# Sweeps over pairs of tiles: 512-column matmuls in place of 256-column ones, with partial sums in joint buffers

## The chip, the cores and the metric

The kernel runs on one core of a Trainium2 chip. A core has five engines with a queue of instructions each: TensorE (PE in the profile, its weight loads PEld), VectorE (DVE), ScalarE (ACT), GpSimd (POOL) and SyncE (SP), which here only issues DMA transfers. TensorE reads SBUF and writes PSUM, whose banks hold 512 float32 columns of 128 partitions. The metric is the device time of one execution in microseconds (us), and the median of several runs is compared.

## What is computed

A chunked linear attention feeds a feed-forward layer. There are 4 batches, 8 heads, 768 positions, a head size of 32 and a state of 16, so 3072 tokens of 256 features reach the second part, which has 2048 hidden features.

```python
for c in range(nc):                       # attention, chunk by chunk
    L = np.exp(cum[:, :, :, None] - cum[:, :, None, :]) * causal
    M = np.einsum('bhin,bhjn->bhij', Cc, Bc) * L
    y[:, :, sl] = M @ xc + np.einsum('bhin,bhnd->bhid', Cc, state) * decay_to_i
    state = decay_full * state + sum_j(Bc[j] * xc[j] * decay_from_j)
x = y.transpose(0, 2, 1, 3).reshape(3072, 256)
h = x @ w_in                              # 256 -> 2048
g = h - np.tanh(h)
out = g @ w_out                           # 2048 -> 256
```

All inputs are float32, except that the two weight matrices come as float64.

## The kernel before

Tokens are columns. The feed-forward part takes them in eight tiles (`WIDTH`, line 31): tiles 0 to 3 have 256 columns, tiles 4 to 7 have 512. The hidden features are 16 blocks f of 128, two to a weight pair u = f // 2.

**A step** (t, f) works on one bank of hidden values. `mm1` (735) computes ph, `act` (773) makes g = ph - tanh(ph) with ScalarE (785) and VectorE (789), and splits g into a rounded part gh (ScalarE, 793) and a rest gl (VectorE, 799). `mm2` (809) multiplies these by the second weights and adds to the output bank or banks `po`. A product of rounded operands is three matmuls, (wh, gh), (wl, gh) and (wh, gl), and in the same way for x in mm1 (755, 831). `blocks(t)` (732) says how many blocks f fit in a bank: for a tile of 256 columns two, so that a step holds 12 matmuls of 256 columns in mm1 and 12 in mm2; for a tile of 512 columns one, and 6 of 512 columns in each. A narrow tile has both output halves e = 0, 1 in the one bank po0; a wide one has them in po0 and po1 (`banks`, 813). Each of the two has one buffer; ph has two (`NPH`).

**Sweeps.** The weights arrive one pair after another and are converted from float64 bits on the way (`conv`). So that work can start early, the narrow tiles are gone through four times (`SWEEPS`, line 53): in the first sweep each takes f = 0 to 3, then each takes 4 to 7, and so on (1075). Partial outputs are put by: after the first sweep `keep` (850) copies the bank into a buffer `pt`, one for each tile; after each later one `add` (863) copies it into a buffer `ob` (two in turn) and an accumulating DMA issued by GpSimd adds that to `pt`. After the last, `store` (875) sends `pt` out in two halves. Tiles 4 to 7 then run all 16 blocks in one go, evicted by ScalarE (e = 0) and VectorE (e = 1). In the first sweep some work runs on unsplit float32 operands (`plain`, `native`: 749, 825).

**Attention.** 28 chunks of up to 112 columns deliver x. Early ones (below `JOINT` = 10) have a bank po1 or po0 for their y (617); later ones come in pairs and take a ph bank (683). Where a chunk is planned is set by `at_` (1093 to 1104). The columns of x lie in a ring: those of tile 5 overwrite those of tiles 0 and 1, so the chunks concerned (12 and 13 first) wait until the last mm1 on the old columns (`over`, 415).

**Order.** Nothing runs as it is written. Each piece of work is recorded with an engine, an estimated cost and its dependencies (`Order`, 59), slots of buffers in the order in which they are asked for. `search` (194 to 207) simulates the whole list 16 times with priorities from the longest remaining path plus a random jitter of fixed seed, and the best order is issued. Mm2 is recorded two steps behind mm1 (`LAG`).

Of the kernel before, what the change touches and what calls it, by code (L numbers as in the profile page):

```python
# [10 lines left out]
F32 = mybir.dt.float32  # L11
# [5 lines left out]
ALU = mybir.AluOpType  # L17
# [3 lines left out]
P = 128  # L21
# [4 lines left out]
NF = FF // P  # L26
# [3 lines left out]
NCK = NB * CPB  # L30
WIDTH = 256, 256, 256, 256, 512, 512, 512, 512
NSW = 4
NT = len(WIDTH)
START = [sum(WIDTH[:t]) for t in range(NT + 1)]
BANK = 512
QLEN = [QL if k >= NCK - NB else Q for k in range(NCK)]
OFF = [sum(QLEN[:k]) for k in range(NCK + 1)]
RING = START[NSW] + WIDTH[NSW]
COL = [START[t] if t <= NSW else START[t] - START[NSW + 1] for t in range(NT)]
CPG = 2  # L40
NG = NCK // CPG
NCONV = NF // 2
# [10 lines left out]
SWEEPS = 0, 2, 4, 6, 8  # L53
# [5 lines left out]
class Order:  # L59
# [1 line left out]


    DMA_LATENCY, SEM, SEM_PE, RATE, FLIGHT = 0.8, 0.15, 0.28, 0.32e6, 8
    ROUNDS, JITTER, SEED, EARLY, LOOK = 16, 0.3, 143, 8.0, 0.5

    def __init__(self):
        self.ops, self.urge = [], []
# [4 lines left out]
    def slot(self, tag, bufs):  # L72
        k = self.count[tag] = self.count.get(tag, -1) + 1
        self.fresh[f"{tag}#{k}"] = tag, f"{tag}#{k - bufs}"
        return f"{tag}#{k}"
# [142 lines left out]
def tile_ssm_moe(ctx: ExitStack, tc: tile.TileContext, a, x, bn, bc, wts, out):  # L218
# [22 lines left out]
    chunks = {t: [k for k in range(NCK) if (START[t] <= OFF[k] or t == 0) and OFF[k] < START[t + 1]] for t in range(NT)}  # L241
    wv, wm, pts, n_pt = {}, {}, {}, {}
    mm1s = {t: [] for t in range(NT)}
    KB = P * 1024

    JOINT = chunks[NSW][0] // CPG * CPG
# [164 lines left out]
    def over(ts, col, w):  # L411

        old = {o for o in range(max(ts)) if max(ts) > NSW and o not in ts and COL[o] < col + w and col < COL[o] + WIDTH[o]}
        assert all(len(mm1s[o]) == NF // blocks(o) for o in old)
        return [i for o in old for i in mm1s[o]]

    def group(G):
# [309 lines left out]


    def rate(w):
        return w * (0.2352 / 512 if 2 * w > BANK else 0.1178 / 256) / 2  # L730

    def blocks(t):
        return BANK // WIDTH[t]

    def mm1(t, f):
        w = WIDTH[t]
        ts = slice(COL[t], COL[t] + w)
        n = [f"x{e}{k}@{t}" for k in range(NCK) if OFF[k] < START[t] + w and OFF[k + 1] > START[t] for e in "hl"]
        n_h, n_g = slot("ph", NPH), slot("g", 3)
        gs[t, f, 0] = [n_h, n_g]  # L740

        def fn():
            ph = ps_h.tile([P, BANK], F32, tag="ph", name=f"ph{t}_{f}")
            gs[t, f] = [ph]
            for i in range(blocks(t)):
                u, j = divmod(f + i, 2)
                if plain(t, f):
                    for k in range(2):
                        nc.tensor.matmul(out=ph[:, i * w : i * w + w], lhsT=part(slice(0, 1), wv[u]).rearrange(  # L749
                                             "p i (k c) -> p (i k) c", k=2)[:, k, j * P : (j + 1) * P],  # L750
                                         rhs=xf[:, k, START[t] : START[t] + w], start=k == 0, stop=k == 1, skip_group_check=True)
                    continue
                for p in range(2):
                    for k in range(2):
                        for w_ in (wh, wl)[: 2 - p]:
                            nc.tensor.matmul(out=ph[:, i * w : i * w + w], lhsT=w_[:, u, 0, k, j * P : (j + 1) * P],  # L756
                                             rhs=(xh, xl)[p][:, k, ts], start=p == 0 and k == 0 and w_ is wh,
                                             stop=p == 1 and k == 1, skip_group_check=True)

        mm1s[t].append(len(op.ops))  # L760
        if plain(t, f):
            n = sorted({"xf" + k[2:] for k in n})
            op("PE", 14.6 * rate(w) * blocks(t), fn, r=[*n, convs[f // 2]], w=[n_h])
            return
        op("PE", 12 * rate(w) * blocks(t), fn, r=[*n, f"wh{f // 2}.0", f"wl{f // 2}.0"], w=[n_h])

# [5 lines left out]

    def act(t, f):
        n_h, n_g = gs[t, f, 0]
        used = WIDTH[t] * blocks(t)
        if native(t, f):
            gs[t, f, 0] += [n_g]
        else:
            n_gh, n_gl = slot("gh", 3), slot("gl", 3)
            gs[t, f, 0] += [n_gh, n_gl]  # L780

        def fn_t():
            g = p3.tile([P, BANK], F32, tag="g", name=f"g{t}_{f}")
            gs[t, f].append(g)
            nc.scalar.activation(g[:, 0:used], gs[t, f][0][:, 0:used], AF.Tanh)  # L785

        def fn_s():
            ph, g = (v[:, 0:used] for v in gs[t, f])
            nc.vector.tensor_tensor(out=g, in0=ph, in1=g, op=ALU.subtract)  # L789

        def fn_h():
            gh = pg.tile([P, BANK], F32R, tag="gh", name=f"gh{t}_{f}")
            nc.scalar.copy(gh[:, 0:used], gs[t, f][1][:, 0:used])  # L793
            gs[t, f].append(gh)

        def fn_l():
            _, g, gh = gs[t, f]
            gl = pg.tile([P, BANK], F32R, tag="gl", name=f"gl{t}_{f}")
            nc.vector.tensor_tensor(out=gl[:, 0:used], in0=g[:, 0:used], in1=gh[:, 0:used].bitcast(F32), op=ALU.subtract)  # L799
            gs[t, f].append(gl)  # L800

        op("ACT", 0.6, fn_t, r=[n_h], w=[n_g])
        op("DVE", 0.69, fn_s, r=[n_h], w=[n_g])
        if native(t, f):
            return
        op("ACT", 0.62, fn_h, r=[n_g], w=[n_gh])
        op("DVE", 0.71, fn_l, r=[n_g, n_gh], w=[n_gl])

    def mm2(t, f, seg):

        w, last = WIDTH[t], f + blocks(t) == seg[1]
        _, _, *n_in = gs[t, f, 0]
        banks = 1 if 2 * w <= BANK else 2
        if f == seg[0]:
# [23 lines left out]
                                             stop=last and k == 2 and i == blocks(t) - 1, skip_group_check=True)  # L838

        if native(t, f):  # L840
            op("PE", 14.5 * rate(w) * blocks(t), fn, r=[*n_in, f"wf{f // 2}"], w=n_po[t, seg])
        else:
            op("PE", 12 * rate(w) * blocks(t), fn, r=[*n_in, f"wh{f // 2}.1", f"wl{f // 2}.1"], w=n_po[t, seg])
        if last:
# [5 lines left out]
    def keep(t, seg):  # L850

        if seg[0]:
            add(t, seg)
            return
        n_pt[t] = slot("pt", NSW)

        def fn():
            pts[t] = p1.tile([P, BANK], F32, tag="pt", name=f"pt{t}", bufs=NSW)
            nc.scalar.copy(pts[t][:, 0 : 2 * WIDTH[t]], po[t, seg][2][:, 0 : 2 * WIDTH[t]])

        op("ACT", 0.6, fn, r=n_po[t, seg], w=[n_pt[t]])

    def add(t, seg):

        name = slot("ob", 2)

        def fn():
            obs[t] = p2.tile([P, BANK], F32, tag="ob", name=f"part{t}_{seg[0]}")
            nc.scalar.copy(obs[t][:, 0 : 2 * WIDTH[t]], po[t, seg][2][:, 0 : 2 * WIDTH[t]])  # L869

        op("ACT", 0.6, fn, r=n_po[t, seg], w=[name])
        op("POOL", 1.0, lambda: nc.gpsimd.dma_start(out=pts[t][:, 0 : 2 * WIDTH[t]], in_=obs[t][:, 0 : 2 * WIDTH[t]],  # L872
                                                   accum_op=ALU.add), r=[name], w=[n_pt[t]])

    def store(t, seg):
        w = WIDTH[t]
        if t < NSW:
            add(t, seg)
            for e in range(2):
                op("SP", 0.42, lambda e=e: nc.sync.dma_start(out=out[e * P : (e + 1) * P, START[t] : START[t] + w],  # L880
                                                             in_=pts[t][:, e * w : e * w + w]), r=[n_pt[t]], dma=KB * w // 256)
            return
        name = op.pieces(slot("ob", 2), 2)

        def fn_c(e):
            if e == 0:
                obs[t] = p2.tile([P, 2, w], F32, tag="ob", name=f"ob{t}")
            if e == 0:
                nc.scalar.copy(obs[t][:, e], po[t, seg][e])
            else:  # L890
                nc.vector.tensor_copy(out=obs[t][:, e], in_=po[t, seg][e])

        def fn_d(e):
            nc.sync.dma_start(out=out[e * P : (e + 1) * P, START[t] : START[t] + w], in_=obs[t][:, e])

        for e in range(2):
            op(("ACT", "DVE")[e], 0.6, lambda e=e: fn_c(e), r=[n_po[t, seg][e]], w=[name[e]])
        for e in range(2):
            op("SP", 0.42, lambda e=e: fn_d(e), r=[name[e]], dma=KB * w // 256)
# [172 lines left out]
    split_x()  # L1072


    segs = [(t, (2 * i, 2 * j)) for i, j in zip(SWEEPS, SWEEPS[1:]) for t in range(NSW)]
    segs += [(t, (0, NF)) for t in range(NSW, NT)]
    steps = [(t, f, seg) for t, seg in segs for f in range(*seg, blocks(t))]
    begin = {}
# [19 lines left out]
    for ck in at_:  # L1098
        if OFF[ck + 1] > START[NSW + 1]:
            for t in range(NSW):  # L1100
                if COL[NSW + 1] <= COL[t] < COL[NSW + 1] + OFF[ck + 1] - START[NSW + 1]:
                    g = max(g for g, step in enumerate(steps) if step[0] == t)
                    for k in range(ck // CPG * CPG, ck + 1):
                        at_[k] = tuple(max(g + 1, v) for v in at_[k])
    for ck in range(len(chunks[0]), NCK):
# [77 lines left out]
```

## Time and profile before

| | us |
|---|---|
| median of 3 runs | 328.02 |
| lowest and highest | 327.78, 328.17 |
| the profiled execution, its time | 328.24 |
| its span, first to last instruction | 326.5 |

The profile comes from the one execution of the third row; what lies around its span is 1.74 us. In the profile's tables "out<-in" names tiles, and L756 is line 756 of the kernel: L749 and L756 are the matmuls of mm1, L825 and L835 those of mm2, L672 and L698 those of a pair of chunks, L631 those of a single chunk, L544 the exponentials, L859 and L869 the evictions of narrow tiles, L872 the accumulating DMA. The chain of work that ended last is followed back from the last instruction, at each step to what released it. Lengths of matmuls overlap, since they are pipelined; what one costs in a row of them is the distance of two starts.

### The profile page before, as it was taken

To read this page: it belongs to the slowest core of one execution; us is meant where nothing else is said; L and a number is where in the kernel's file an instruction comes from. 1 tells how busy PE (TensorE), PEld (TensorE's weight loads), DVE (VectorE), ACT (ScalarE), POOL (GpSimd) and SP (SyncE) were. 2 spreads that over 40 slices of the span, in tenths; PEclk is the share of its full clock that TensorE was granted. 3 is DMA by queue.
4 is the path that set the end of the run, shared out by engine and by line. 5 is a ranking of instruction groups with operands and counts; after the bars stand their busy time and mean duration, and the time that the engine had idled before them with its cause. 6 is when DMAs were issued, how large, how long until landed. Compare 5 with 4: busy or idle time off the path is not lost.

```text
span 326.5 us, 6317 instructions
## 1 busy us (share of the span) xinstructions
PE 318.3 (97%) x2448; PEld 270.8 (83%) x2448; DVE 217.1 (66%) x314; ACT 210.6 (65%) x471; POOL 65.6 (20%) x94
## 2 busy tenths in 40 slices
PE   8988999999999999999999999999999999999994
PEld 7856887899999999887887887887878888888883
DVE  6979987888989776465564565564766555545551
ACT  6567879567788767685766756475958544534451
POOL 8614455001324321240211202010202000000000
PEclk9999999999999999999999999999999999999999
DMA  6659666659232192280605105005430000200001
GB/s 201 222 175 323 199 225 241 205 182 332 46 53 48 32 280 45 41 251 2 220 2 161 44 2 185 22 1 168 159 108 2 0 0 2 79 0 2 0 0 64
DMA packets 16029, 35.30 MB, mean 108 GB/s; under 512 B 2528, under 2 KB 5504, under 8 KB 16000
## 3 DMA queue, kind: packets, MB, share of 16 engines
q1 hardware_dynamic: 14272, 31.76, 28.8%
q0 software_dynamic: 1728, 3.15, 5.7%
q8 instruction: 19, 0.31, 0.4%
q14 instruction: 10, 0.08, 0.1%
HBM read 28.32 MB, written 3.43 MB: 97 GB/s over the span
## 4 chain that ended last, share of the span: by engine, by line
PE 91%; DVE 5%; ACT 2%; issue 1%; DVEq 0%
PE ph L756 39%; PE o L835 38%; PE o L825 4%; PE y L698 3%; PE att L672 3%; DVE lt L465 1%; PE warm L986 1%; PE y L631 1%; DVE wm L332 1%; ACT lt L544 1%; PE att L506 1%; PE ph L749 1%; DVE parts L1029 0%; DVE wv L329 0%; PE att L501 0%
## 5 line engine op out<-in xcount | busy, mean ns | idle before, releaser
L789 DVE TENSOR_TENSOR g<-ph,g 128x512 f32<-128x512 f32 x96 | 65.8, 687 | 50.1 <-ACT g L785 49.7
L785 ACT ACTIVATE g<-ph 128x512 f32<-128x512 f32 x96 | 57.4, 598 | 51.0 <-PE ph L756 50.9
L799 DVE TENSOR_TENSOR gl<-g,gh 128x512 fp32r<-128x512 f32 x88 | 64.5, 734 | 33.9 <-ACT gh L793 32.6
L756 PE MATMUL ph<-xh,wh 128*128 128x512 f32 (+1 forms) x248 | 82.2, 342 | 0.0
L756 PE MATMUL ph<-xh,wl 128*128 128x512 f32 (+1 forms) x248 | 81.2, 338 | 0.0
L793 ACT CAST gh<-g 128x512 fp32r<-128x512 f32 x88 | 54.5, 619 | 29.9 <-DVE g L789 28.7
L835 PE MATMUL o<-gh,wh 128*128 128x512 f32 (+1 forms) x224 | 66.0, 347 | 0.0
L835 PE MATMUL o<-gl,wh 128*128 128x512 f32 (+1 forms) x224 | 65.3, 344 | 0.0
L835 PE MATMUL o<-gh,wl 128*128 128x512 f32 (+1 forms) x224 | 65.3, 344 | 0.0
L756 PE MATMUL ph<-xl,wh 128*128 128x512 f32 (+1 forms) x248 | 63.5, 338 | 0.0
L756 PEld LDWEIGHTS ph<-xh,wh 128*128 128x128 f32 x248 | 47.0, 190 | 5.6 <-issue 0.4
L756 PEld LDWEIGHTS ph<-xh,wl 128*128 128x128 f32 x248 | 47.0, 190 | 5.0
L526 POOL TENSOR_SCALAR_AFFINE_SELECT lt<-lt 128x896 f32<-128x896 f32 (+1 forms) x24 | 27.6, 1149 | 113.5 <-ACT lt L544 104.0
L756 PEld LDWEIGHTS ph<-xl,wh 128*128 128x128 f32 x248 | 42.7, 190 | 5.0
L835 PEld LDWEIGHTS o<-gh,wh 128*128 128x128 f32 x224 | 37.3, 189 | 6.2 <-issue 0.8
L544 ACT ACTIVATE lt<-lt,ncum 128x112 f32<-128x112 f32 (+1 forms) x144 | 41.6, 375 | 0.0
L835 PEld LDWEIGHTS o<-gl,wh 128*128 128x128 f32 x224 | 37.3, 190 | 5.1
L835 PEld LDWEIGHTS o<-gh,wl 128*128 128x128 f32 x224 | 37.3, 189 | 4.8
L872 POOL DMA_DIRECT2D pt<-part x12 | 10.6, 880 | 56.7 <-ACT part L869 56.7
L678 DVE TENSOR_TENSOR lt<-att,lt 128x896 f32<-128x896 f32 (+1 forms) x18 | 18.7, 1049 | 0.0
L825 PE MATMUL o<-g,wf 128*128 128x256 f32 x64 | 15.7, 389 | 0.7 <-DVE g L789 0.7
L825 PEld LDWEIGHTS o<-g,wf 128*128 128x128 f32 x64 | 11.5, 190 | 3.3 <-DVE g L789 0.9
(97 smaller groups left out, 272.7 us busy)
## 6 DMA issues: line engine op xcount, KB each, us to landing
lt<-cumr SPq DMA_DIRECT2D x18, 512.0 KB
raw<-w_d SPq DMA_DIRECT2D x16, 512.0 KB
bc<-bc_d SPq DMA_DIRECT2D x14, 352.0 KB
x<-x_d SPq DMA_DIRECT2D x14, 256.0 KB
pt<-part POOLq DMA_DIRECT2D x12, 256.0 KB, 4.1
out_d<-ob SPq DMA_DIRECT2D x8, 256.0 KB
braw<-bn_d SPq DMA_DIRECT2D x14, 112.0 KB
out_d<-pt SPq DMA_DIRECT2D x8, 128.0 KB
```

Of the source, the lines that this page charges most:

```text
L526: nc.gpsimd.affine_select(out=k["l"][:, :, 0:q], in_=k["l"][:, :, 0:q], pattern=[[0, H], [1, q]], compare_op=ALU.is_ge, fill=0.0, base=N, ...
L544: nc.scalar.activation(k["l"][:, h, 0:q], k["l"][:, h, 0:q], AF.Exp, bias=ncum[:, h, ck : ck + 1])
L672: nc.tensor.matmul(out=a_[:, i], lhsT=bb[r], rhs=cc[r, :, 0 : qlen(ck)], start=True, stop=True)
L678: nc.vector.tensor_tensor(out=l, in0=chs[j]["a"], in1=l, op=ALU.mult)
L756: nc.tensor.matmul(out=ph[:, i * w : i * w + w], lhsT=w_[:, u, 0, k, j * P : (j + 1) * P], rhs=(xh, xl)[p][:, k, ts], start=p == 0 and k = ...
L785: nc.scalar.activation(g[:, 0:used], gs[t, f][0][:, 0:used], AF.Tanh)
L789: nc.vector.tensor_tensor(out=g, in0=ph, in1=g, op=ALU.subtract)
L793: nc.scalar.copy(gh[:, 0:used], gs[t, f][1][:, 0:used])
L799: nc.vector.tensor_tensor(out=gl[:, 0:used], in0=g[:, 0:used], in1=gh[:, 0:used].bitcast(F32), op=ALU.subtract)
L825: nc.tensor.matmul(out=po[t, seg][e], lhsT=wf[:, u, 256 * j + e * P : 256 * j + (e + 1) * P], rhs=gs[t, f][1][:, i * w : i * w + w], start ...
L835: nc.tensor.matmul(out=po[t, seg][e], lhsT=w_[:, u, 1, j, e * P : (e + 1) * P], rhs=g[:, i * w : i * w + w], start=f == seg[0] and k == 0 ...
L872: op("POOL", 1.0, lambda: nc.gpsimd.dma_start(out=pts[t][:, 0 : 2 * WIDTH[t]], in_=obs[t][:, 0 : 2 * WIDTH[t]], accum_op=ALU.add), r=[name ...
```

## The change

From the second sweep on the narrow tiles are taken as two wide ones, number 8 (tiles 0 and 1) and number 9 (tiles 2 and 3), of 512 columns, with one block f to a step and both output banks. The number of steps stays. The first sweep stays as it was, but its partial sums go to two buffers `pt` of two halves e, 512 columns each, and each tile writes its 256 columns of both halves. A wide tile's `add` takes one bank at a time, each with its own copy and its own accumulating DMA, and `store` sends 512 columns per half. `left` counts the blocks that each old tile still has to do, for the ring. The estimated costs and the seed of the search differ as well.

```diff
-    ROUNDS, JITTER, SEED, EARLY, LOOK = 16, 0.3, 143, 8.0, 0.5
+    ROUNDS, JITTER, SEED, EARLY, LOOK = 16, 0.3, 266, 8.0, 0.5
...
+NM = NSW // 2
+WIDE = WIDTH + tuple(sum(WIDTH[2 * m : 2 * m + 2]) for m in range(NM))
+FROM = START[:NT] + START[0:NSW:2]
+AT = COL + COL[0:NSW:2]
+OF = [[t] for t in range(NT)] + [[2 * m, 2 * m + 1] for m in range(NM)]
...
-        assert all(len(mm1s[o]) == NF // blocks(o) for o in old)
+        assert not any(left[o] for o in old)
...
     def rate(w):
-        return w * (0.2352 / 512 if 2 * w > BANK else 0.1178 / 256) / 2
+        return w * (0.227 / 512 if 2 * w > BANK else 0.12 / 256) / 2
 
     def blocks(t):
-        return BANK // WIDTH[t]
+        return BANK // WIDE[t]
 
     def mm1(t, f):
-        w = WIDTH[t]
-        ts = slice(COL[t], COL[t] + w)
+        w = WIDE[t]
+        ts = slice(AT[t], AT[t] + w)
...
-        mm1s[t].append(len(op.ops))
+        for o in OF[t]:
+            mm1s[o].append(len(op.ops))
+            left[o] -= blocks(t)
...
     def keep(t, seg):
 
         if seg[0]:
             add(t, seg)
             return
-        n_pt[t] = slot("pt", NSW)
+        m, i = divmod(t, 2)
+        if i == 0:
+            op.pieces(slot("pt", NM), 2)
+        n_pt[t] = f"pt#{m}.{i}"
 
         def fn():
-            pts[t] = p1.tile([P, BANK], F32, tag="pt", name=f"pt{t}", bufs=NSW)
-            nc.scalar.copy(pts[t][:, 0 : 2 * WIDTH[t]], po[t, seg][2][:, 0 : 2 * WIDTH[t]])
+            if i == 0:
+                pts[m] = p1.tile([P, 2, BANK], F32, tag="pt", name=f"pt{m}", bufs=NM)
+            nc.scalar.copy(pts[m][:, :, i * BANK // 2 : (i + 1) * BANK // 2],
+                           po[t, seg][2][:, 0 : 2 * WIDTH[t]].rearrange("p (e w) -> p e w", e=2))
 
     def add(t, seg):
 
-        name = slot("ob", 2)
-
-        def fn():
-            obs[t] = p2.tile([P, BANK], F32, tag="ob", name=f"part{t}_{seg[0]}")
-            nc.scalar.copy(obs[t][:, 0 : 2 * WIDTH[t]], po[t, seg][2][:, 0 : 2 * WIDTH[t]])
-
-        op("ACT", 0.6, fn, r=n_po[t, seg], w=[name])
-        op("POOL", 1.0, lambda: nc.gpsimd.dma_start(out=pts[t][:, 0 : 2 * WIDTH[t]], in_=obs[t][:, 0 : 2 * WIDTH[t]],
-                                                   accum_op=ALU.add), r=[name], w=[n_pt[t]])
+        m = t - NT
+        for e in range(2):
+            name = slot("ob", 2)
+
+            def fn(e=e):
+                obs[t, e] = p2.tile([P, BANK], F32, tag="ob", name=f"part{t}_{seg[0]}_{e}")
+                nc.scalar.copy(obs[t, e], po[t, seg][e])
+
+            op("ACT", 0.6, fn, r=[n_po[t, seg][e]], w=[name])
+            op("POOL", 1.0, lambda e=e: nc.gpsimd.dma_start(out=pts[m][:, e], in_=obs[t, e], accum_op=ALU.add),
+               r=[name, n_pt[2 * m], n_pt[2 * m + 1]], w=[f"sum{m}.{e}"])
 
     def store(t, seg):
-        w = WIDTH[t]
-        if t < NSW:
+        w = WIDE[t]
+        if t >= NT:
             add(t, seg)
+            m = t - NT
             for e in range(2):
-                op("SP", 0.42, lambda e=e: nc.sync.dma_start(out=out[e * P : (e + 1) * P, START[t] : START[t] + w],
-                                                             in_=pts[t][:, e * w : e * w + w]), r=[n_pt[t]], dma=KB * w // 256)
+                op("SP", 0.42, lambda e=e: nc.sync.dma_start(out=out[e * P : (e + 1) * P, FROM[t] : FROM[t] + w], in_=pts[m][:, e]),
+                   r=[f"sum{m}.{e}"], dma=KB * w // 256)
             return
...
-    segs = [(t, (2 * i, 2 * j)) for i, j in zip(SWEEPS, SWEEPS[1:]) for t in range(NSW)]
+    segs = [(t, (2 * i, 2 * j)) for i, j in zip(SWEEPS, SWEEPS[1:]) for t in (range(NT, NT + NM) if i else range(NSW))]
...
-                    g = max(g for g, step in enumerate(steps) if step[0] == t)
+                    g = max(g for g, step in enumerate(steps) if t in OF[step[0]])
```

## What I predict

> **What bounds the kernel now.** I read the page's totals first, then the granted clock, then busy time by stretches, then the chain that ended last.
>
> ```profile
> span 326.5 us, 6317 instructions
> PE 318.3 (97%) x2448; PEld 270.8 (83%) x2448; DVE 217.1 (66%) x314; ACT 210.6 (65%) x471; POOL 65.6 (20%) x94
> core 0: 326.5 us, clock 0.999
> core 0: us, PE busy (x) PEld busy (x) DVE busy (x) ACT busy (x) POOL busy (x), PEclk, DMA share, GB/s
> 0.00:27.27 27.27, 23.83 (x321) 18.73 (x321) 21.93 (x43) 17.32 (x32) 15.08 (x33) 1.00 0.66 209
> 27.27:61.22 33.95, 33.28 (x409) 26.93 (x409) 29.69 (x38) 26.76 (x70) 14.39 (x14) 1.00 0.65 220
> 61.22:84.00 22.78, 22.78 (x185) 22.57 (x185) 19.58 (x27) 15.35 (x25) 2.37 (x3) 1.00 0.77 252
> 84.00:107.00 23.00, 23.00 (x194) 23.00 (x193) 20.73 (x26) 19.77 (x47) 8.62 (x10) 1.00 0.28 47
> 107.00:137.15 30.15, 30.15 (x275) 28.92 (x273) 20.41 (x31) 19.78 (x43) 7.54 (x9) 1.00 0.44 108
> 137.15:322.48 185.33, 185.29 (x1076) 150.68 (x1076) 104.09 (x152) 111.68 (x256) 17.62 (x25) 1.00 0.19 62
> ```
>
> From 61.22 to 322.48 us the busy time of PE is the length of the stretch: TensorE never pauses there. A busy PE need not be fast, so whether this stretch can shrink is a question of how closely its matmuls follow each other. The last column but two is the granted clock: full everywhere, nothing to gain or lose there. 61.22 to 137.15 is the stretch of sweeps two to four, the only one whose matmuls the change touches; I cut it in three to see how near VectorE comes to the limit.
>
> In the chain each row is a start, a length and a run of instructions. Its rows from that stretch, one from before it, and two from the late tiles, which are 512 columns wide already:
>
> ```profile
> 51.14 0.52 PE y L631 x16
> ...
> 61.22 1.62 PE ph L756 x12
> 62.85 1.73 PE o L825 x8
> 64.58 2.88 PE ph L756 x24
> 67.45 1.44 PE o L835 x12
> 68.89 1.44 PE ph L756 x12
> ...
> 113.53 0.97 PE att L672 x16
> 114.50 1.01 PE y L698 x32
> 115.51 3.06 PE o L835 x24
> ...
> 131.53 2.75 PE ph L756 x12
> 134.28 2.87 PE o L835 x24
> ...
> 306.12 1.36 PE ph L756 x6
> 307.48 1.36 PE o L835 x6
> ```
>
> A narrow group, twelve matmuls of 256 columns, takes 1.44 us; a wide group, six of 512, does the same arithmetic in 1.36. The single instructions say it too (start, length, engine and form; the lengths overlap, so the starts are what counts):
>
> ```profile
> 64.65 0.28 PE L756 MATMUL ph<-xh,wh 128*128 128x256 f32 x1
> 64.77 0.28 PE L756 MATMUL ph<-xh,wl 128*128 128x256 f32 x1
> 320.24 0.39 PE L835 MATMUL o<-gh,wh 128*128 128x512 f32 x1
> 320.46 0.39 PE L835 MATMUL o<-gh,wl 128*128 128x512 f32 x1
> ```
>
> Narrow ones start 0.12 us apart; wide ones 0.22 by these rounded starts, 1.36/6 = 0.227 by the group. Two narrow take 0.240, one wide 0.227: a matmul less is worth 13.3 ns.
>
> **The change part by part.**
>
> *Matmuls.* How many groups become wide comes from the table of forms:
>
> ```profile
> L756 PE MATMUL ph<-xh,wh 128*128 128x256 f32 x120 | 32.3, 290 | 0.0
> L835 PE MATMUL o<-gh,wh 128*128 128x256 f32 x96 | 15.5, 284 | 0.0
> ```
>
> A narrow mm1 holds four of the first and a narrow mm2 four of the second: 120/4 = 30 mm1 groups and 96/4 = 24 mm2 groups. Six of the 30 belong to tiles 1 to 3 in the first sweep (three tiles of two steps) and stay; the second sweep on has 3 sweeps x 4 tiles x 2 steps = 24 of each. So 48 groups go from 1.44 to 1.36 us: 48 x 0.08 = 3.84 us. The stretch closes on this: 48 x 1.44 = 69.12, one first-sweep mm2 1.73, the pair of chunks at 113.53 1.98, two wide mm1 of tile 4 2.75, and 0.19 and 0.18 that the first group after such small matmuls costs extra (1.62 and 3.06 above against 1.44 and 2.88), together 75.95 of 75.93. Nothing else lies in it, so 3.84 is all that this part can give, and all of it is on the path.
>
> *Rule against row.* The Trainium skill's page "TensorE: Matmul & The Clock Gate", section "Wait — 56ns, not 53.3ns?", puts matmuls that follow each other at full clock N / 2.4 GHz plus about 2.5 ns apart. By that, 288 matmuls less would be an estimated 0.72 us. This trace disagrees: its narrow ones stand 120 ns apart, where the rule says 109, and its wide ones 227, where it says 216.
>
> *The elementwise work* of a step (L785, L789, L793, L799) stays: a step still fills 512 columns of ph, once per step, 24 steps. Cost nothing.
>
> *Evictions and partial sums.* Rows of the stretch, then the tile's DMA times, then one batch of exponentials that can stand ahead on ScalarE:
>
> ```profile
> L869 ACT COPY part<-o 128x512 f32<-128x512 f32 x11 | 6.4, 586 | 6.1 <-PE o L835 6.0
> L872 POOL DMA_DIRECT2D pt<-part x11 | 9.7, 881 | 52.4 <-ACT part L869 52.4
> DMA to landing us min/median/max: 3.3/4.1/8.8
> 96.84 2.33 ACT L544 ACTIVATE lt<-lt,ncum 128x112 f32<-128x112 f32 x8
> ```
>
> Before: 12 narrow evictions, one per tile and sweep (one falls just outside the stretch). After: 6 wide tiles with two banks each, again 12 copies of 128x512 and 12 accumulating DMAs. Equal count, equal size; they now come in pairs every four steps (4 x 2.72 = 10.88 us) instead of one every two (5.76). Three covers are to be checked. *(a) The bank.* mm2 of the next tile waits for the copies. A bank-0 copy can begin while bank 1 is still being filled (0.68 us), and at least one mm1 of 1.36 lies between; after the group's end it takes 0.59 for the copy of bank 1. Cover 1.36 against 0.59 and two handovers: no cost, unless ScalarE is in the middle of a batch of 2.33. Behind a waiting copy on ScalarE stand tanh and gh of the next steps, which PE needs. *(b) The two ob buffers.* Each is reused after 10.88 us, before after 11.52. Needed: 0.59 copy, up to two issues of 0.88, 4.1 to landing, 6.5 in all; with the longest landing 11.2, which the 1.36 of (a) still covers. The 6.0 us that L869 waited were for PE, none for a buffer. *(c) POOL.* The second issue holds POOL 0.88 us longer in one piece; L526 and L547 queue behind it. POOL is busy 18.5 of 75.93 us (the three rows above), so nothing.
> The first-sweep copies L859 now write two runs of 256 columns. No row has that form; it can cost from 0 to a second copy, 0.6 us each, four times. I take 0, since ScalarE has idle time around them.
>
> *Stores.* Eight stores of 128 KB become four of 256 KB on SP, long before the end, which hangs on tile 7. Nothing; four issues go.
>
> *Moved waits.* A wide mm2 finishes e = 0 before e = 1, so gl is read by its third matmul, 0.45 us in, instead of the ninth, 0.96 in. The late tiles (137 to 322) run in that order with no pause. Weight pair u = 3, 5, 7 is first used one step later, 2.72 us of slack gained. Chunks 12 and 13 write ring columns of tiles 0 and 1 and may be placed two steps later, 5.4 us; tile 4 wants them at 131.53, and they ran at 113.53, so 12.6 us remain. The first wide mm2 needs bank 1, which the last chunk with a y of its own (at 51.14) leaves some 16 us earlier than that mm2's turn (67.45). No cost.
>
> *Order.* Two rates and the seed differ, so the whole order is searched anew. Where PE never pauses that can't help. In the first 61 us it can:
>
> ```profile
> 14.32 1.01 DVE wm L332
> 25.14 1.36 DVE wm L332
> ```
>
> Here the chain runs over VectorE, and 0.67 us of PE idle remain even from 27.27 on. One weight operation put before or behind one of a chunk moves the start by 1.01 to 1.36 us. I take 0 and keep 1.36 to both sides.
>
> **Sum.** The profiled execution took 328.24 us, 1.74 around its span. Less 3.84: 324.4. The median shown is 328.02, 0.22 below it, so 324.2.
>
> **The rivals.** About 0.2% (0.66 us) is what a measurement of this kernel can tell from no change.
>
> 1. *VectorE takes over.* From 84 to 107 it is busy 20.73 of 23.00 us, 90%; 16 wide groups would do this in 21.72, 95%. If its 2.27 us of gaps (waits for ScalarE's half of each step) can't shrink, this stretch keeps its length and 1.28 are lost: 325.5. If the same held from 61 on (45.78 us, some 31 groups) 2.5 would go: 326.7. For it: both engines serve the same step in turn. Against: PE has no gap, weight conversions are not urgent and gained a step, and over the whole stretch VectorE goes only from 60.7/75.9 to 60.7/72.1, 84%.
> 2. *The start falls otherwise*, by 1.36: 325.5 if worse, 322.8 if better.
> 3. *The 13.3 ns belong to the stretch, not to the width*: then the change doesn't do what it says, wide groups there take 1.44, and 328.0 stays. For it: the weight loader is busy 23.00 of 23.00 us among narrow groups and 81% later (150.68 of 185.33). Against: two wide mm1 stand inside the stretch, at 131.53, and took 2.75. (Under the skill's rule the gain of 0.72 would give 327.3; the trace has spoken against its 2.5 ns.)
> 4. *Slower: turns that wait for the eviction.* Place: the first mm2 of each wide tile, six times. If a batch of 2.33 us stands ahead of the copies on ScalarE, they end 0.59 + 2.33 = 2.9 us after the group, 1.6 later than the one mm1 lasts. From three such turns on (4.8) it eats the gain and ends slower than before: 329.0; six make 9.6, less 3.84, 333.8. For it: four of these batches lie in the stretch, and now both banks must be emptied, where bank 1 was idle. Against: eleven narrow turns with the same ScalarE queue and no PE pause, and the wide turns of the late tiles, on both banks with one copy on ScalarE and one on VectorE, have none either.
>
> **How the numbers follow.** Forecast 324.2, itself 323.5 to 324.9: 0.64. Rival 1: 0.15, mostly its lower price. Rival 2: 0.06 better, 0.06 worse. Rival 3: 0.03. Rival 4: 0.06, of which 0.05 slower and 0.01 no change. Faster 0.64 + 0.15 + 0.12 = 0.91, same 0.03 + 0.01 = 0.04, slower 0.05. The range goes from 322.8, the better start, to 326.0, which takes in the worse start and the lower price of rival 1; it leaves out the rest of rival 1 (0.05) and rivals 3 and 4, 0.14 in all.
>
> **What would show it.** Right: no form 128x256 left at L835's place; groups of six in 1.36 us from about 61 us on; PE busy equal to the stretch; 24 wide mm1 and 24 wide mm2 more; the first mm1 of tile 4 about 3.8 us earlier, all after it shifted alike. Rival 1 shows as PE idle behind VectorE's g or gl between 61 and 107, rival 2 as a first narrow group that ends earlier or later than before while the sweeps still shrink by 3.84, rival 3 as six matmuls in 1.44, rival 4 as PE idle released by the copy of part at the turns. I am wrong if two of these losses meet, or if the new order leaves chunk work among the late tiles that now sits in the start.

## The result, and the profile after

The changed kernel takes 323.91 us (median; 323.79 to 324.25), the kernel before 327.9 in the same set: ratio 0.9879, 95% interval 0.9862 to 0.9896. The forecast was 324.2 and 322.8 to 326.0.

The totals of the page of the changed kernel, its busy time by stretches (length, then busy time of each engine, granted clock, DMA) and its matmuls by form:

```profile
span 322.6 us, 5757 instructions
PE 313.7 (97%) x2160; PEld 255.3 (79%) x2160; DVE 215.3 (67%) x314; ACT 210.3 (65%) x471; POOL 60.6 (19%) x94
```

```profile
0.00:61.18 61.18, 56.12 (x729) 45.44 (x729) 51.20 (x80) 43.76 (x102) 24.91 (x47) 1.00 0.66 215
61.18:133.42 72.24, 72.24 (x361) 59.17 (x360) 58.27 (x81) 56.21 (x120) 18.26 (x22) 1.00 0.51 136
133.42:318.75 185.33, 185.32 (x1077) 150.69 (x1076) 105.13 (x153) 110.33 (x249) 17.40 (x25) 1.00 0.20 64
318.75:322.60 3.85, 0.00 (x0) 0.00 (x0) 0.69 (x1) 0.00 (x0) 0.00 (x0) 1.00 0.36 136
```

```profile
L844 PE MATMUL o<-gh,wh 128*128 128x512 f32 x176 | 69.2, 393 | 0.0
L763 PE MATMUL ph<-xh,wh 128*128 128x512 f32 x176 | 69.1, 393 | 0.0
...
L763 PE MATMUL ph<-xh,wh 128*128 128x256 f32 x24 | 6.9, 307 | 0.0
```

L763 and L844 are the lines of mm1 and mm2 now. 2160 matmul records in place of 2448 are 288 fewer, six for each of the 48 groups that were counted. No form of 256 columns is left at mm2's line 844, and of mm1's 24 in each of three forms stay, the six groups of the first sweep. Against the stretches of before:

| stretch | before | after | difference |
|---|---|---|---|
| to the first group of the second sweep | 61.22 | 61.18 | -0.04 |
| sweeps two to four | 75.93 | 72.24 | -3.69 |
| late tiles | 185.33 | 185.33 | 0.00 |
| after the last matmul | 4.02 | 3.85 | -0.17 |
| span | 326.5 | 322.6 | -3.9 |

So the time went where it was looked for. The chain through that stretch:

```profile
61.18 1.59 PE ph L763 x6
62.77 1.73 PE o L834 x8
64.50 2.78 PE ph L763 x12
67.28 1.36 PE o L844 x6
...
76.80 2.72 PE ph L763 x12
...
118.22 1.59 PE o L844 x6
119.80 1.38 PE ph L763 x6
...
132.06 1.36 PE o L844 x6
```

Every group of six takes 1.36, but for those right behind smaller matmuls. 48 x 0.08 = 3.84 were expected and 3.69 measured; the rest is at the seams: a wide first group behind small matmuls takes 1.59, 0.23 more than the usual, where a narrow one took 0.18 to 0.19 more, and 2.78 and 1.38 add 0.08. Together 0.54 of extras against 0.38 of before (with 2.75 there), 0.16 given back.

### The profile page after: what moved, and what is told of

Same layout as the page of the kernel before. It is cut to its first block, busy times and chain, and to the rows that moved or that the text cites. A ratio compares the mean times of both kernels' runs of the same rounds, so it can differ in the third digit from the quotient of the medians.

```text
span 322.6 us, 5757 instructions
## 1 busy us (share of the span) xinstructions
PE 313.7 (97%) x2160; PEld 255.3 (79%) x2160; DVE 215.3 (67%) x314; ACT 210.3 (65%) x471; POOL 60.6 (19%) x94
## 4 chain that ended last, share of the span: by engine, by line
PE 91%; DVE 5%; ACT 2%; issue 1%
PE ph L763 39%; PE o L844 38%; PE o L834 3%; PE y L704 3%; PE att L678 3%; PE y L637 1%; PE warm L1003 1%; DVE lt L471 1%; ACT lt L550 1%; DVE lt L520 1%; DVE wv L345 1%; PE att L461 1%; PE cp L451 1%; ACT lt L516 1%; DVE wm L338 1%
## 5 line engine op out<-in xcount | busy, mean ns | idle before, releaser
L763 PE MATMUL ph<-xh,wh 128*128 128x512 f32 (+1 forms) x200 | 76.0, 382 | 0.0
L763 PE MATMUL ph<-xh,wl 128*128 128x512 f32 (+1 forms) x200 | 74.8, 377 | 0.0
L844 PE MATMUL o<-gh,wh 128*128 128x512 f32 x176 | 69.2, 393 | 0.0
L844 PE MATMUL o<-gl,wh 128*128 128x512 f32 x176 | 68.5, 389 | 0.0
L844 PE MATMUL o<-gh,wl 128*128 128x512 f32 x176 | 68.5, 389 | 0.0
L763 PE MATMUL ph<-xl,wh 128*128 128x512 f32 (+1 forms) x200 | 59.0, 376 | 0.0
L763 PEld LDWEIGHTS ph<-xh,wh 128*128 128x128 f32 x200 | 37.6, 188 | 7.6 <-issue 0.6
L763 PEld LDWEIGHTS ph<-xh,wl 128*128 128x128 f32 x200 | 37.6, 188 | 6.8
L763 PEld LDWEIGHTS ph<-xl,wh 128*128 128x128 f32 x200 | 36.7, 188 | 7.0
L844 PEld LDWEIGHTS o<-gh,wh 128*128 128x128 f32 x176 | 33.0, 188 | 7.8 <-issue 0.8
L844 PEld LDWEIGHTS o<-gl,wh 128*128 128x128 f32 x176 | 33.0, 188 | 6.9
L844 PEld LDWEIGHTS o<-gh,wl 128*128 128x128 f32 x176 | 33.1, 188 | 6.7
L834 PE MATMUL o<-g,wf 128*128 128x256 f32 x64 | 15.4, 384 | 1.4 <-ACT x L578 0.9
L605 ACT CAST xh<-y 128x224 fp32r<-128x224 f32 (+4 forms) x18 | 7.3, 413 | 13.1 <-DVE s L711 10.6
```

Of the source, the lines that this page charges most:

```text
L834: nc.tensor.matmul(out=po[t, seg][e], lhsT=wf[:, u, 256 * j + e * P : 256 * j + (e + 1) * P], rhs=gs[t, f][1][:, i * w : i * w + w], start ...
L844: nc.tensor.matmul(out=po[t, seg][e], lhsT=w_[:, u, 1, j, e * P : (e + 1) * P], rhs=g[:, i * w : i * w + w], start=f == seg[0] and k == 0 ...
```

## The experiments

Theory: the gain is 288 matmuls of 13.3 ns each on an engine that never waits in the sweeps. Rivals: the new order, VectorE's nearness to its limit, waits at the turns of the wide tiles.

### The wide matmuls cut up again

In `halves_sweeps` each matmul of tiles 8 and 9 is issued in two halves with the same weights, all else and every order kept. The cut of mm1 is shown, shortened; that of mm2 is alike. `unequal_sweeps` cuts at column 384, `quarters_sweeps` into four, and `halves_tail` halves those of tiles 4 to 7 instead.

```diff
+    def cut_up(t, w):
+        return [(0, 256), (256, 512)] if t >= NT else [(0, w)]
...
+    for lo, hi in cut_up(t, w):
-        nc.tensor.matmul(out=ph[:, i * w : i * w + w], lhsT=..., rhs=(xh, xl)[p][:, k, ts], ...)
+        nc.tensor.matmul(out=ph[:, i * w + lo : i * w + hi], lhsT=..., rhs=(xh, xl)[p][:, k, ts.start + lo : ts.start + hi], ...)
```

> The changed kernel, every order of work kept, but each 512-column matmul of the wide tiles 8 and 9 issued as two of 256 columns with the same weights: 288 matmuls more. Theory (each matmul costs a fixed 13.3 ns beside its columns): six wide become 1.44 us again, 288 x 0.0133 = 3.84 more than 323.9, 327.7. Rival (the gain came from the order that was searched anew): 323.9 stays. If the fixed part were 2.5 ns: 324.6.

> The changed kernel with the matmuls of the late tiles 4 to 7 cut into halves of 256 columns and the sweeps left wide: 768 matmuls more, in a stretch in which VectorE is busy little more than half of the time. Theory of a cost per matmul: 768 x 0.0133 = 10.2 more than 323.9, 334.1. Rival (the 13.3 ns belong to the stretch of the sweeps with its busy weight loader and VectorE): 323.9 to 326.

`halves_sweeps` took 328.01 (326.63 to 328.81), beside 328.17 for the kernel before in its set, ratio 0.9979 (0.9951 to 1.0008): all of the gain is gone, with the new order and the joint buffers still in place. Its chain (start, length, instructions):

```profile
61.45 1.63 PE ph L767 x12
...
64.81 2.88 PE ph L767 x24
67.69 1.44 PE o L850 x12
...
135.97 1.43 PE o L850 x12
137.40 0.97 PE att L678 x16
```

61.45 to 137.40 is 75.95 us, the 75.93 of the kernel before. `halves_tail` took 334.65 (333.84 to 335.84), 10.7 above 323.91 where 10.2 were expected. The late tiles take 194.97 in place of 185.33 between the same points, 9.64 more, and 0.86 arose at the start (62.04 in place of 61.18), which this cut does not touch; in the traces of the kernels that keep the changed kernel's order this point lies anywhere from 60.08 (`copies_twice`) to 62.04:

```profile
62.04 1.58 PE ph L767 x6
...
134.47 0.97 PE att L678 x16
...
323.67 5.77 PE o L850 x48
```

So the 13.3 ns are no property of the sweeps: 9.64 over 768 matmuls is 12.6 ns each, in a stretch in which VectorE is idle four tenths of the time (105.13 busy of 185.33 in the changed kernel). Each piece also loads its weights again (3024 loads for 3024 matmuls in `quarters_sweeps`, 2160 for 2160 in the changed kernel), so these runs price a matmul together with its weight load; which of the two the 13.3 ns belong to stays open.

> As before, but each wide matmul is cut into 384 and 128 columns. The number of matmuls is that of the halves, the columns too. Theory of a fixed part per matmul: again 327.7. Rival (among narrow groups the weight load sets the pace: one takes 0.12 us, and a matmul can't follow the last one sooner): 384 columns take 0.173, 128 take 0.120 in place of 0.067, so 0.293 in place of 0.227 for 512, 288 x 0.066 = 19 more than 323.9, 343.

> The changed kernel, order kept, each wide matmul of the sweeps cut into four of 128 columns: 864 matmuls more. A fixed part of 13.3 ns per matmul and nothing else: 4 x 0.067 = 0.267 for 512 columns, 288 x 0.040 = 11.5 more than 323.9, 335. A floor of 0.114 us per matmul whose weights are loaded anew, as the cut into 384 and 128 suggests (0.287 less 0.173): 4 x 0.114 = 0.456, 288 x 0.229 = 66 more, 390.

```profile
67.81 1.72 PE o L850 x12
69.53 1.72 PE ph L767 x12
```

```profile
70.28 2.68 PE o L850 x24
72.96 2.68 PE ph L767 x24
```

The first pair of rows is `unequal_sweeps` (340.94 us; 340.89 to 341.37), the second `quarters_sweeps` (one run, 386.74). Six pieces of 384 with six of 128 take 1.72, which is 0.287 a pair; 24 of 128 take 2.68, 0.112 each. A fixed part alone would give 0.240 and 0.067. Both fit a floor: such a matmul, with weights of 128 x 128, does not follow the last one sooner than some 0.112 us. For 0.287 less 0.112 is 0.175, and 384 columns at the pace of the wide ones (0.227 less 13.3 ns is 213.3 for 512 columns, three quarters of it 160, and 13.3 again) would take 0.173. The expectations of 343 with a floor of 0.120 and of 390 with one of 0.114 were both somewhat too high; that there is a floor was right. The narrow matmuls of before, at 0.120, lay just above it. It is no floor of every matmul: the small ones of attention, with weights of 128 x 32 (0.52 for 16 in the chain of before) or 32 x 128 (0.97 for 16), follow each other faster.

What makes the floor, the runs show only in part. In `quarters_sweeps` the weight loader is busy all of the time from 64.97 to 142.64 us (77.67 of 77.67), but every matmul here loads its own weights, and none was run without. The Trainium skill's page "TensorE: Matmul & The Clock Gate", section "LDWEIGHTS (loading the stationary operand)", puts a load at the number of weight columns / 1.2 ns, 107 ns for 128, which comes near the 112 measured.

### The order

`after_old_order` is the changed kernel with the rates, the two unsplit costs and the seed of before, `before_new_order` the kernel before with those of the changed one; `after_seed_143` and `after_seed_29` change only the seed. From the edit of `after_old_order`, without the two unsplit costs:

```diff
-    ROUNDS, JITTER, SEED, EARLY, LOOK = 16, 0.3, 266, 8.0, 0.5
+    ROUNDS, JITTER, SEED, EARLY, LOOK = 16, 0.3, 143, 8.0, 0.5
...
-        return w * (0.227 / 512 if 2 * w > BANK else 0.12 / 256) / 2
+        return w * (0.2352 / 512 if 2 * w > BANK else 0.1178 / 256) / 2
```

> The changed kernel with the rates and the seed of before, so the order is another one. Theory (the gain is in the matmuls; the order moves only the first 61 us, by at most 1.36): 322.6 to 325.3, the sweeps as long as in the changed kernel within 0.3. Rival (the new order brought the gain): near 328.

> The kernel before with the rates and the seed of the changed one: narrow sweeps in another order. Theory (the sweeps owe their length to the matmuls, the order decides about the start only): from 61 us on as in the kernel before, the start up to 3.4 us later, as the order of before cost the changed kernel, since this seed wasn't picked for this kernel: 327 to 331. Rival (the new rates and seed are the gain, whatever the matmuls): 324.

> The changed kernel with only the seed of before, the new rates kept. Old rates and old seed together made it 327.5 by a later start. If it was the seed, that is an order drawn without picking, this one lies 1 to 4 us over 323.9, 325 to 328, with the sweeps as long as in the changed kernel. If it was the rates: 323.9.

> A third seed, the one of 40 whose planned order is longest. If orders drawn without picking cost up to some 4 us at the start, 326 to 328.5; if the order is of no account, 323.9.

> The changed kernel as it is, beside the two other orders of this set on one chip. 323.9 within 0.7.

Each ratio is to the kernel before in the same set of runs.

| kernel | order | median (range), us | ratio to before (95%) |
|---|---|---|---|
| before | its own | 327.9 | 1 |
| before | rates and seed of after | 330.33 (329.13 to 331.27) | 1.0071 (1.005 to 1.0092) |
| after | its own, run again | 323.93 (323.71 to 324.04) | 0.9879 (0.9864 to 0.9893) |
| after | rates and seed of before | 327.5 (324.97 to 328.22) | 0.9958 (0.9921 to 0.9996) |
| after | seed 143 | 326.66 (326.15 to 328.44) | 0.9969 (0.9955 to 0.9984) |
| after | seed 29 | 329.48 (329.23 to 330.88) | 1.0056 (1.0036 to 1.0077) |

The expectation for `after_old_order` (at most 325.3) was missed by 2.2 us, that for `after_seed_29` (at most 328.5) by 1.0. Where these lie is in the chain. The first group of the second sweep, what of the first sweep still follows it, and the end of the sweeps, of `after_old_order`:

```profile
62.87 1.58 PE ph L763 x6
64.46 1.73 PE o L834 x8
...
67.58 1.73 PE o L834 x8
...
136.85 0.97 PE att L678 x16
```

and of `after_seed_29`:

```profile
64.39 1.60 PE ph L763 x6
66.00 1.73 PE o L834 x8
...
69.10 1.73 PE o L834 x8
...
138.36 0.97 PE att L678 x16
```

Two groups of L834 are left over here, one in the changed kernel, so 1.73 us more of the first sweep's work stand inside the stretch. 136.85 - 62.87 - 1.73 = 72.25, and 138.36 - 64.39 - 1.73 = 72.24: the sweeps are as long as in the changed kernel (72.24) whatever the order. The start is 62.87 + 1.73 - 61.18 = 3.42 us later in the one and 4.94 in the other. The theory of the sweeps stands; the size that I gave to the start does not. `after_seed_143` shows that the seed alone does this: with the new rates its sweeps last 72.22 by the same count (135.58 - 61.63 - 1.73), and they begin 2.18 us later. `before_new_order`, the narrow kernel, shows the other half of the table:

```profile
61.99 1.62 PE ph L756 x12
...
66.78 1.73 PE o L825 x8
...
138.20 0.97 PE att L672 x16
...
140.18 1.62 PE o L835 x12
```

From 61.99 to the end of the last narrow group at 141.80 (140.18 and 1.62) it is 79.81; without the second L825, the pair of chunks that here comes before the last narrow group (1.98) and the 0.18 that this group then costs extra, 75.92, the length of before. With seed and rates equal on both sides the widening reads as -0.7 us in total (328.17 to 327.5, one set) or as -6.4 (330.33 to 323.93, two sets), and in the sweeps it is -3.7 both times.

### VectorE's room

`dve_half` makes gl twice in every second step of the wide tiles, `dve_full` in every step.

```diff
+            for _ in range(2 if t >= NT and f % 2 else 1):
                 nc.vector.tensor_tensor(out=gl[:, 0:used], in0=g[:, 0:used], in1=gh[:, 0:used].bitcast(F32), op=ALU.subtract)
```

> The changed kernel, order kept, the subtraction that makes gl done twice in every second step of the wide tiles: 12 more of 0.6 to 0.7 us, 7 to 8 us more on VectorE in 72.25. Theory (PE sets the pace with VectorE at 58.3 of 72.25, 81%): 66 of 72.25, at most 1 us of waits, 323.9 to 325. Rival (VectorE already set the pace in part): the whole 7 to 8, 331.

> The same in every step: 24 more, 14.4 to 16.8 us. VectorE then has 72.7 to 75 us of work for 72.25: it becomes the bound. Theory: PE waits for g or gl in the sweeps, 1 to 6 us longer than 323.9, 325 to 330. If it stays at 324, VectorE has more room than its busy time says.

The sweeps' stretch of each, `dve_half` and then `dve_full` (PE, its weight loads, VectorE, ScalarE, GpSimd):

```profile
61.12:134.56 73.44, 72.83 (x360) 58.94 (x360) 66.65 (x93) 55.74 (x120) 18.33 (x22) 1.00 0.50 133
```

```profile
61.38:139.53 78.15, 74.27 (x360) 58.43 (x360) 74.14 (x105) 55.83 (x120) 18.96 (x22) 1.00 0.47 125
```

They took 325.18 (324.77 to 326.48) and 330.11 (329.88 to 330.69), 1.3 and 6.2 more, in the sweeps 1.20 and 5.91 more; both lie just above what was expected (325 and 330). 8.4 us of added work cost 1.2, the next 7.5 cost 4.7. Of `dve_full`, what PE's loader waited for most in that stretch (us, times, longest):

```profile
PEld ph L763 <- DVE g L798: 4.1, 4, 2.4
PEld o L845 <- DVE gl L809: 3.0, 5, 1.2
```

An mm1 waits for a ph bank that g's subtraction frees, an mm2 for gl. This is the rival that I had given 0.15: its waits look like this. As a mean over the sweeps they begin somewhere between 81% of VectorE's time (58.27 of 72.24, no wait of PE) and 91% (66.65 of 73.44). The share alone does not decide, though. Here are the changed kernel where the rival was looked for, and the start of the sweeps of `after_old_order`:

```profile
84.00:107.00 23.00, 23.00 (x103) 19.04 (x102) 20.10 (x26) 19.31 (x42) 7.17 (x9) 1.00 0.28 48
```

```profile
62.87:84.00 21.13, 21.13 (x95) 17.62 (x95) 20.24 (x27) 13.81 (x22) 2.47 (x3) 1.00 0.67 222
```

In the first VectorE is busy 87% of the time, where the rival had reckoned with 95%; in the second 96%, and PE does not pause there either.

### The turns

`copies_twice` evicts every bank twice.

```diff
                 nc.scalar.copy(obs[t, e], po[t, seg][e])
+                nc.scalar.copy(obs[t, e], po[t, seg][e])
```

> The changed kernel, order kept, each eviction of a wide tile's bank done twice: 12 copies of 0.59 us more on ScalarE, 1.17 us more at each turn of a wide tile. Theory (at each turn two mm1, 2.72 us, lie between the last mm2 of one tile and the first of the next, and the copies are through 0.6 to 1.3 us after the first): 1.8 to 2.5 of 2.72 used, PE does not wait, 323.9 to 324.4. Rival (the turns stand just at the edge): about 1 us at each of five turns, 329.

It took 324.48 (323.55 to 324.84), where at most 324.4 was expected. Its sweeps last 72.61 (60.08 to 132.69), 0.37 more. The weight loader has one wait there that the changed kernel lacks:

```profile
92.08 0.19 PEld L763 LDWEIGHTS ph<-xh,wh 128*128 128x128 f32 x1 [0.49 <-DVE g L798]
```

The chain says how it came about:

```profile
87.37 0.60 ACT part L885
...
88.48 2.34 ACT lt L550 x8
90.82 0.49 ACT g L794
91.34 0.70 DVE g L798
92.08 3.02 PE ph L763 x12
```

The copies pushed a batch of exponentials back, that pushed a tanh back, and an mm1 waited for its ph bank, which the subtraction after that tanh frees. No output bank was late. The turns have room for twice the copies; the 0.37 came by ScalarE's queue, where tanh stands behind copies and exponentials.

## Why the prediction was right, point by point

**The bound.** PE without a pause from the second sweep to the end, at full clock: so it is after (72.24 of 72.24, 185.32 of 185.33). With that the elementwise work, the stores and the moved waits cost nothing either, as said.

**The matmuls.** 48 groups, 0.08 each: right, 3.69 of 3.84, and the halves give it back in place and in the late tiles. The step "a matmul less is worth 13.3 ns" holds for 512, 384 and 256 columns; at 128 each costs 0.112 and not 0.067. It did not bear on this change. The 2.5 ns of the Trainium skill (page "TensorE: Matmul & The Clock Gate", section "Wait — 56ns, not 53.3ns?") would have given an estimated 0.7; 3.69 were measured, so the row decides.

**Evictions and turns.** No cost, as said, with a wider cover than I took: at every turn the order has two mm1 between the last mm2 of a tile and the first of the next, 2.72 us and not 1.36. ScalarE's row for the copies shows that nothing but 0.2 us of idle time stood before them, so they waited for no ob buffer; and PE's stretch without a pause says that no mm2 waited for a bank:

```profile
L885 ACT COPY part<-o 128x512 f32<-128x512 f32 x11 | 6.1, 589 | 0.2
```

The first-sweep copies of two runs of columns cost 0.59 each, as those of before did, so nothing extra was right. The accumulating DMAs held POOL for 1.06 us each in the median in place of 0.87, and took 4.5 to landing in place of 4.1; the covers took that in.

**VectorE.** Right, with a little more room than reckoned: 81% in the stretch in place of 84%, no wait. As a mean over the stretch the margin is less than 10 points.

**The order.** Here a size was off. "I take 0 and keep 1.36 to both sides": the 0 came out (-0.04), but four other orders of these kernels cost 2.5 (329.0 against 326.5 of span, `before_new_order`) to 5.5 us (329.48 against 323.93). An order of the changed kernel that fell as unluckily as seed 29 would have made it slower than before. I priced one weight operation misplaced on VectorE. In the chain of `after_seed_29` up to 61 us VectorE has 26.9 us, 15.6 of them weight operations, against 15.5 and 6.6 in the changed kernel. But the chain of `after_old_order` has only 6.8 and 1.5, and that of `before_new_order` stands behind a transfer of weights for 6 us:

```profile
18.62 6.00 DMA raw<-w_d
```

So the bad orders are late in different ways, which were not taken apart; a price that three of them share, in the clock, comes at the end. The forecast was met because both kernels' own orders begin the second sweep at the same time with the same work left (61.22 and 61.18). That was luck: nothing in the profile of before could have told it, and in the traces of the kernels that share one order this point lies anywhere within 2 us (60.08 to 62.04). The slower side of the prediction should have hung on this term and not on the turns.

**Rivals 3 and 4** did not occur. Of the orders run, the changed kernel's own is the fastest.

## What to carry to other kernels

On an engine that never waits, count the instructions: where the profile holds both forms of the same work, their distance in a row of equal groups priced the change here to 0.15 us (3.84 against 3.69). Before widening on that, see whether the narrow form already sits at a floor like the 0.112 us here, since then the gain is far larger (four matmuls of 128 columns take 0.447 us, one of 512 takes 0.227), and how much room the engine beside it has, since that is what a faster engine uses up. Where a search with a seed makes the order, compare stretches and not totals: the draw moved the total by more (323.93 to 329.48) than the change did (327.9 to 323.91).

## What the hardware showed that was not expected

The clock took part in the price of a bad order. Rows by stretches of `after_old_order`, the granted clock third from the end, and the same work twice in its chain:

```profile
26.00:28.00 2.00, 0.97 (x64) 0.97 (x65) 1.12 (x3) 1.97 (x5) 1.27 (x3) 1.00 0.91 270
28.00:30.00 2.00, 0.54 (x8) 0.54 (x11) 2.00 (x4) 1.55 (x6) 0.52 (x1) 0.89 0.87 272
30.00:32.00 2.00, 2.00 (x11) 1.26 (x8) 2.00 (x4) 1.83 (x5) 1.20 (x2) 0.50 1.01 316
```

```profile
22.75 1.94 PE ph L756 x8
...
30.70 3.07 PE ph L756 x8
```

For four microseconds TensorE was busy 1.51 of 4.00, with one pause of 2.07 for VectorE; then its clock was halved, and eight matmuls took 3.07 in place of 1.94. A wait at the start can thus be paid for twice. The trace of `after_seed_29` has two pauses of 1.81 and a clock of 0.50 behind each, that of `before_new_order` one of 2.23 and a clock of 0.58. No drop shows where the longest pause of the first 61 us was 1.40 (`after_seed_143`) or 0.86 (the changed kernel, 1.00 throughout); so the 2.18 us of `after_seed_143` are no matter of the clock. In `after_old_order` it is much of the miss: the one of its ten executions with a mean granted clock of 1.000 took 324.97 us, inside what was expected, and the nine at 0.987 to 0.995 took 326.91 to 328.22. And lastly, a first group behind small matmuls costs 0.23 us when it is wide and 0.18 when it is narrow; why, no run settles.
